# The memory turn of a recurrent attention kernel in two parts, with its sum copied on ScalarE, and another choice of streamed weight blocks

## The chip, the cores and the metric

The kernel runs on one core of a Trainium2 chip. The metric is the device time of one execution in microseconds (us), the median of several runs. The engines are TensorE (PE; its weight loads are PEld), VectorE (DVE), ScalarE (ACT), GpSimd (POOL) and SyncE (SP), which here only issues transfers. Tensors in HBM reach the on-chip memory SBUF by DMA; matmul results lie in PSUM until ACT or DVE copies them out.

## The reference

Two attention branches read the same `x` (2048 tokens, 640 wide) and a gate mixes them. Branch A is causal attention with 32 heads of 20 over a window of 256. Branch B is what the change touches: 64 segments of 32 tokens, one after the other, each with 8 memory tokens that the segment before has left.

```python
for s in range(n_seg):                       # 64, seg_len 32
    xs = x[:, s*seg_len:(s+1)*seg_len, :]
    h = concatenate([mem, xs], axis=1)       # 8 + 32 tokens
    q, k, v = h @ Wq, h @ Wk, h @ Wv         # 640 -> 32 heads x 192
    p = softmax(where(mask, q k^T * scale, -1e9))
    o = einsum('bhte,hed->btd', p v, Wo)     # back to 640
    mem = o[:, :M, :]                        # M = 8
    outs.append(o[:, M:, :])
return g * a + (1 - g) * concatenate(outs)   # g = sigmoid(sum(x * gate_w))
```

Only the memory ties a segment to the next, so branch B is a chain of 64 steps.

## The kernel before

Branch A runs first. In the same stretch and just after it the kernel projects the last eight tokens of each segment for q, k and v (class `Tail`), and loads weights. Then `branch_B` runs the 64 segments.

The four weights of branch B hold 84 blocks: for q, k and v four head groups of five blocks (one per slice `kt` of the 640 inputs, 128 x 1536 bf16, 384 KB), for the output projection o four groups of six (128 x 1280, 320 KB). [...] The table `STREAMED` names 21 blocks that are read from HBM again in every segment; the other 63 stay resident. A streamed block lands in a slot of the ring `b_w`, which has `RING = 5` slots. The load of a block is issued by SP once the last matmul on the block five places earlier has ended. SP issues the loads in the order of their use (`Weights.load`, L517 for blocks that are one transfer, L521 for o blocks 0, 2, 3 and 5; blocks 1 and 4 of o would be two).

Each segment follows the list `STEP` on PE, which is written out by hand: `k0 q0 k1 tk0 tq0 q1 s0 ... v3 p3 oa2 pv3 ob2 oa3 ob3 m`. `k0`, `q0`, `v0` are projections of a head group (`chunk`, L773; five slices `kt` of four matmuls that run side by side), `tk`/`tq` turns of the tokens, `s` scores, `p` the turn of the probabilities, `pv` the values (L935, L942), `oa`/`ob` two halves of an output group (L968), and `m` the memory turn. `Sched.run` plans the other engines from durations and dependences; SP and PE keep the given order.

At a segment's end stands this chain. The output sum of the segment lies in PSUM (`o_b`). DVE copies it to SBUF (`osum`, a buffer of the tag `OT`, L977). In `finish`, ten small matmuls turn the memory tokens (L989, `mem_ps`). DVE copies the result into the eight memory columns of the next segment's input `hT` (L994). Then `k0` of the next segment starts (L773). POOL stores the rest of `osum`, loads the branch A share and writes the output; `mix` runs on DVE in the next segment.

Of the kernel before, what the change touches and what calls it, by code (L numbers as in the profile page):

```python
# [8 lines left out]
FP32 = mybir.dt.float32  # L9
BF = mybir.dt.bfloat16  # L10
ALU = mybir.AluOpType
ACT = mybir.ActivationFunctionType
# [3 lines left out]
MEM = 8  # L16
# [377 lines left out]
P = 128  # L394
KT = 5
D = 640
# [273 lines left out]
def branch_B(ctx, tc, xin, mem0, weights, ring, c, omg_sb, ga_dram, b_dram, outf, hold, held, rest):  # L670
    nc = tc.nc
    nseg = xin.shape[0]
    scale = float(192) ** -0.5
    still, ident, mask, mk_m, mk_x, mk_z = c.still, c.ident, c.mask, c.mk_m, c.mk_x, c.mk_z
    kept = KEPT

    sb = {
        "w": (RING, [P, PIECE]), "tok": (3, [P, 384]), "vtok": (1, [P, 384]), "K02": (1, [P, 4, 2, L]),
        "PTm": (1, [P, 2, 4, L]), "Pm": (1, [P, 4, SEG]), "xg": (2, [P, 2, 12, MEM]), "xv": (1, [P, 384]), "hT": (2, [P, KT, SEG]),
# [6 lines left out]
    sc = Sched({"rest": len(held)} | {t: n for t, (n, _) in sb.items()} | {t: n for t, (n, _) in kept.items()} | ps)  # L686

    def tile_of(b, shape=None, dtype=BF, name=None):
        t = b["tag"]
        if b["tile"] is None:  # L690
            if t in kept:
                b["tile"] = still[t][b["n"] % kept[t][0]]
            elif t in sb:
                b["tile"] = pools[t].tile(sb[t][1], BF, name=f"b_{t}", tag=t)
            else:
                b["tile"] = pools[t].tile(shape, dtype, name=name or f"p_{t}", tag=t)
        return b["tile"]

    def load_x(s):
        hb = sc.buf("hT")  # L700

        def f():
            nc.gpsimd.dma_start(tile_of(hb)[:].rearrange("p k t -> p (k t)"), xin[s, :, 0:KT * SEG])
        return hb, sc.op("POOL", 540, 5000, f, writes=[hb])
# [16 lines left out]
    def pieces(kind, g, ms=range(5)):  # L721

        out = {}
        for m in ms:
            u = (kind, g, m)
            if u in weights.streamed:
                b = out[m] = sc.buf("w")
                sc.op("SP", 0.753 * weights.width(kind), 3000, lambda b=b, u=u: weights.load(u, tile_of(b)[:, 0:weights.width(u[0])], nc.sync), writes=[b])
        return out

    def w_of(kind, g, m, bufs):
        return bufs[m]["tile"] if m in bufs else weights.tiles[kind, g, m]
# [15 lines left out]
    hts = {0: load_x(0)}  # L748
# [3 lines left out]
    def f_m0():  # L752
        t = tile_of(tp, [P, KT, MEM], BF, "tp0")
        for kt in range(KT):
# [4 lines left out]
          writes=[hts[0][0]], after=[hts[0][1]])  # L759
# [192 lines left out]
    def oproj(kind, s, g):  # L952

        ms = PARTS[kind]
        OT = made["O", s, g]
        if g == 0 and kind == "oa":
            obufs[s] = sc.buf("o")
        o_b = obufs[s]
        wb = pieces("o", g, ms)

        def f(m):
            t = tile_of(o_b, [P, 512], FP32, "ps_o")
            for n in range(2):
                i, b = divmod(2 * m + n, 3)
                c = (4 * b + i) * L
                for h in range(2):
                    w = w_of("o", g, m, wb)[:, n * D + h * (D // 2):n * D + (h + 1) * (D // 2)]
                    nc.tensor.matmul(t[64 * h:64 * h + 64, 0:D // 2], lhsT=OT["tile"][:, c:c + 64], rhs=w,  # L968
                                     start=(g == 0 and m == 0 and n == 0), stop=(g == 3 and m == 5 and n == 1),
                                     tile_position=(0, 64 * h), skip_group_check=True)  # L970
        for m in ms:
            sc.op("PE", 273, 200, lambda m=m: f(m), reads=[OT] + [wb[n] for n in wb if n == m] + [slow[u] for u in slow if s == 0 and u == ("o", g, m)],
                  writes=[o_b], name=("o", s, g, m), mode=64)
        if g < 3 or kind == "oa":
            return
        osum = sc.buf("OT")
        sc.op("DVE", 492, 55, lambda: nc.vector.tensor_copy(tile_of(osum)[:, 0:D // 2], o_b["tile"][:, 0:D // 2]), reads=[o_b], writes=[osum])  # L977
        made["osum", s] = osum

    def finish(s):  # L980

        osum = made.pop(("osum", s))
        b = sc.buf("tr")

        def f():
            t = tile_of(b, [P, KT, MEM], FP32, "mem_ps")
            for kt in range(KT):
                for h in range(2):
                    nc.tensor.matmul(t[64 * h:64 * h + 64, kt, :], lhsT=osum["tile"][:, kt:D // 2:KT], rhs=ident[:, 64 * h:64 * h + MEM],  # L989
                                     start=(kt == 0), stop=True, tile_position=(0, 64 * h), skip_group_check=True)  # L990
        sc.op("PE", 360, 222, f, reads=[osum], writes=[b], name=("m", s), mode=64)
        if s + 1 < nseg:
            hT, xl = hts[s + 1]
            sc.op("DVE", 200, 55, lambda: nc.vector.tensor_copy(tile_of(hT)[:, :, 0:MEM], b["tile"][:]), reads=[b], writes=[hT], after=[xl])  # L994
        ga, rows = sc.buf("ga"), slice(s * SEG, (s + 1) * SEG)
        half = lambda t, h: t[rows, h * (D // 2):(h + 1) * (D // 2)]
        mine = lambda t, h: t[64 * h + MEM:64 * h + L, 0:D // 2]
        for h in range(2):
            sc.op("POOL", 500, 3000, lambda h=h: nc.gpsimd.dma_start(half(b_dram, h), mine(osum["tile"], h)), reads=[osum])
            sc.op("POOL", 500, 5000, lambda h=h: nc.gpsimd.dma_start(mine(tile_of(ga), h), half(ga_dram, h)), writes=[ga])  # L1000

        def mix(after):
            def f_r():
                nc.vector.scalar_tensor_tensor(out=ga["tile"][:], in0=osum["tile"][:, 0:D // 2], scalar=omg_sb[:, s:s + 1], in1=ga["tile"][:],  # L1004
                                               op0=ALU.mult, op1=ALU.add)
            sc.op("DVE", 552, 60, f_r, reads=[osum], writes=[ga], after=[after])
            for h in range(2):
                sc.op("POOL", 500, 3000, lambda h=h: nc.gpsimd.dma_start(half(outf, h), mine(tile_of(ga), h)), reads=[ga])  # L1008
        made["mix"] = mix
        if s + 1 == nseg:  # L1010
            mix(None)
# [3 lines left out]
    for n in names:  # L1015
        kind, s = n[:2]
        if s not in tails:
            tails[s] = load_tail(s)
            if s + 1 < nseg:
                hts[s + 1] = load_x(s + 1)  # L1020
        if kind == "m":
            finish(s)
        elif kind in "qkv":
            chunk(kind, s, n[2])
        elif kind in PARTS:
            oproj(kind, s, n[2])
        else:
            make[kind](s, n[2])
    with tc.manual_schedule():
        parts = []  # L1030
        for n in names:
            if n[0] in PARTS:
                parts += [("o",) + n[1:] + (m,) for m in PARTS[n[0]]]
            elif n[0] in KINDS:
                parts += [n + (m,) for m in range(KT)]
            else:
                parts.append(n)
        return sc.run([("m0", 0)] + parts)


PARTS = {"oa": range(3), "ob": range(3, 6)}
RING = 5
EARLY = 24
LAST = 11
HOLD = 5
DENSE = 8
STREAMED = {"q": ((1,), (1,), (2,), (1,)),
            "k": ((0,), (3,), (3,), (3,)),
            "v": ((4,), (0, 4), (0, 3), (3,)),
            "o": ((2,), (2, 5), (0, 3), (2, 5))}  # L1050


@with_exitstack
def kernel(
# [31 lines left out]
    allp = [(k, g, m) for k in KINDS for g in range(4) for m in range(6 if k == "o" else 5)]  # L1086
    streamed = [(k, g, m) for k, g, m in allp if m in STREAMED[k][g]]
    weights = Weights(tc, B_Wq, B_Wk, B_Wv, B_Wo, streamed)
# [6 lines left out]
    units = [lambda u=u: weights.load_resident(pre, u, nc.sync) for u in early]  # L1095
    ring = wctx.enter_context(tc.tile_pool(name="b_w", bufs=RING))
    first = {}
# [78 lines left out]
    with ExitStack() as bctx:  # L1176
        rest = bctx.enter_context(tc.tile_pool(name="b_rest", bufs=1))
        branch_B(bctx, tc, xin, mem0, weights, ring, step_c, omg_sb, ga_dram, b_dram, outf, holds[0], last[HOLD:], rest)
# [41 lines left out]
```

## Time and profile before

| | |
|---|---|
| median of 5 runs | 2080.93 us (2071.89 to 2084.55) |
| the profiled execution | 2063.62 us, its span 2061.9 us |
| busy: PE, DVE, ACT, POOL | 1915.6, 1047.9, 920.5, 727.2 us |
| first and last start of the memory copy L994 | 466.8 and 2029.5 us, 63 copies |
| moved by DMA | 593.83 MB, mean 288 GB/s over the span |

The segments fill the span from about 440 us on. PE is busy for 93% of the span, but its matmuls are pipelined and their ends are modelled, so this is no statement that PE works at its peak. The waits that count are those of PE; DVE, ACT and POOL are idle for half the time. One loop of the chain from copy L994 to the next takes (2029.5 - 466.8) / 62 = 25.2 us.

### The profile page before, as it was taken

Reading aid. Unit: us, or ns where it says so; the run is one execution under the profiler, and the core shown is the slowest. Engines: PE = TensorE matmul, PEld = TensorE weight load, DVE = VectorE, ACT = ScalarE, POOL = GpSimd, SP = SyncE. Lnnn points to the kernel's source line nnn. Section 1 sums busy time; section 2 is a strip of 40 time slices with the busy share of each in tenths; the row PEclk is TensorE's granted clock in tenths of the full one; section 3 lists DMA queues with packets and bytes.
Section 4 is the critical chain, followed back from the end, with each engine's and each line's share of the span. In section 5 each row is a group of like instructions: output and inputs, shape, how many; then the busy total and the mean of one; then the engine's idle time right before and its main releaser. Section 6 shows DMA issues by size and latency. Waiting matters only on the chain.

```text
span 2061.9 us, 92142 instructions
## 1 busy us (share of the span) xinstructions
PE 1915.6 (93%) x39670; PEld 1409.8 (68%) x39670; DVE 1047.9 (51%) x3338; ACT 920.5 (45%) x1885; POOL 727.2 (35%) x2008
## 2 busy tenths in 40 slices
PE   7999999989999999999999999999999999999997
PEld 6878878756666666666666666666666666666665
DVE  4888853334444445444445544444444444444444
ACT  3888832234444444444444444444444443444443
POOL 4222121233333334333343333333333333333332
PEclk8999999999999999999999999999999999999999
DMA  4232139789999999999999999999999999999997
GB/s 138 78 88 72 45 96 351 203 274 317 328 335 329 332 336 337 331 324 326 334 335 336 337 339 332 330 332 333 330 327 333 330 332 306 332 323 332 335 330 261
DMA packets 251153, 593.83 MB, mean 288 GB/s; under 512 B 39528, under 2 KB 59120, under 8 KB 250736
## 3 DMA queue, kind: packets, MB, share of 16 engines
q1 hardware_dynamic: 219248, 540.07, 75.2%
q0 software_dynamic: 31488, 47.78, 8.7%
q8 instruction: 313, 5.13, 1.0%
q14 instruction: 104, 0.85, 0.1%
HBM read 558.33 MB, written 29.37 MB: 285 GB/s over the span
## 4 chain that ended last, share of the span: by engine, by line
PE 60%; DMA 24%; issue 7%; DVE 5%; ACT 3%; SPq 0%; POOL 0%; POOLq 0%; DVEq 0%; ACTq 0%
DMA b_w<-in_B_Wo_dram 11%; PE ps_q L773 10%; PE ps_k L773 10%; DMA b_w<-in_B_Wv_dram 9%; PE ps_o L968 8%; PE ps_v L773 6%; PE t_psum L584 4%; PE qk_ps L138 3%; PE t_psv L602 2%; DMA b_w<-in_B_Wk_dram 2%; PE tr_q L797 2%; PE S_ps L853 2%; PE tr_k L797 2%; PE s_ps L236 2%; PE ps_pv L935 2%
## 5 line engine op out<-in xcount | busy, mean ns | idle before, releaser
L773 PEld LDWEIGHTS <-b_hT 128*32 128x32 bf16 x15360 | 372.6, 96 | 263.6 <-issue 50.6
L968 PEld LDWEIGHTS <-b_OT 128*64 128x64 bf16 x6144 | 370.4, 110 | 57.2 <-issue 32.5
L784 ACT CAST b_tok<-ps_k 128x384 bf16<-128x384 f32 x256 | 122.6, 479 | 340.4 <-PE ps_k L773 331.8
L773 PE MATMUL ps_q<-w_q,b_hT 128*32 128x384 bf16 x4096 | 257.4, 329 | 0.8 <-issue 0.8
L773 PE MATMUL ps_k<-w_k,b_hT 128*32 128x384 bf16 x4096 | 245.5, 328 | 0.0
L968 PE MATMUL ps_o<-hold,b_OT 128*64 128x320 bf16 x2560 | 237.4, 301 | 0.0
L919 DVE TENSOR_TENSOR b_PTm<-PT_ps,marks 128x320 bf16<-128x320 f32 x256 | 125.9, 492 | 201.1 <-PE PT_ps L907 201.1
L968 PE MATMUL ps_o<-b_w,b_OT 128*64 128x320 bf16 x1792 | 206.5, 301 | 23.0 <-DMA b_w<-in_B_Wo_dram 21.3
L824 DVE TENSOR_TENSOR b_Kz<-tr_k,marks 128x256 bf16<-128x256 bf16 x256 | 108.1, 422 | 230.7 <-PE tr_k L797 223.2
L773 PE MATMUL ps_v<-w_v,b_hT 128*32 128x384 bf16 x3584 | 212.4, 327 | 0.0
L239 ACT ACTIVATE pt<-s_ps 128x1024 bf16<-128x1024 f32 x180 | 183.6, 1026 | 57.3 <-PE s_ps L236 54.1
L946 ACT CAST b_OT<-ps_pv 128x480 bf16<-128x480 f32 x256 | 143.2, 559 | 143.4 <-PE ps_pv L942 143.4
L784 ACT CAST b_vtok<-ps_v 128x384 bf16<-128x384 f32 x256 | 122.7, 479 | 153.4 <-PE ps_v L773 152.7
L718 POOL DMA_DIRECT2D b_xg<-xin x256 | 142.5, 557 | 83.8 <-POOL b_QT L810 51.7
L968 PE MATMUL ps_o<-w_o,b_OT 128*64 128x320 bf16 x1792 | 169.9, 300 | 0.0
L829 POOL COPY b_K<-b_xg 128x64 bf16<-128x64 bf16 x256 | 61.0, 238 | 298.6 <-PE S_ps L853 298.6
L806 ACT COPY b_QT<-tr_q 128x384 bf16<-128x384 bf16 x256 | 123.5, 483 | 86.5 <-PE tr_q L797 86.5
L784 ACT CAST b_tok<-ps_q 128x384 bf16<-128x384 f32 x256 | 123.1, 481 | 84.8 <-PE ps_q L773 84.7
L773 PE MATMUL ps_v<-b_w,b_hT 128*32 128x384 bf16 x1536 | 131.2, 331 | 25.7 <-DMA b_w<-in_B_Wv_dram 24.5
L1008 POOL DMA_DIRECT2D out_dram<-b_ga x128 | 63.7, 498 | 256.2 <-DVE b_ga L1004 246.4
L977 DVE CAST b_OT<-ps_o 128x320 bf16<-128x320 f32 x64 | 31.5, 492 | 210.2 <-issue 201.5
L797 PEld LDWEIGHTS <-b_tok 128*64 128x64 bf16 x3072 | 108.3, 110 | 41.1 <-issue 22.4
(141 smaller groups left out, 3715.8 us busy)
## 6 DMA issues: line engine op xcount, KB each, us to landing
b_w<-in_B_Wv_dram SPq DMA_DIRECT2D x384, 384.0 KB, 4.9
b_w<-in_B_Wo_dram SPq DMA_DIRECT2D x448, 320.0 KB, 4.7
b_w<-in_B_Wk_dram SPq DMA_DIRECT2D x256, 384.0 KB, 4.9
b_w<-in_B_Wq_dram SPq DMA_DIRECT2D x256, 384.0 KB, 5.0
xin<-hold POOLq DMA_DIRECT2D x8, 1536.0 KB, 12.3
b_xg<-xin POOLq DMA_DIRECT2D x256, 48.0 KB, 4.4
w_q<-in_B_Wq_dram SPq DMA_DIRECT2D x16, 384.0 KB, 3.9
w_k<-in_B_Wk_dram SPq DMA_DIRECT2D x16, 384.0 KB, 3.9
```

The source lines that it names most:

```text
L239: nc.scalar.activation(out=pt, in_=sp[:], func=ACT.Exp, scale=scale)
L584: self.nc.tensor.matmul(pt[:, bb, :], lhsT=w[kt][:, c:c + P], rhs=self.xTb[:, kt, t0:t0 + hs * MEM], start=(kt == 0), stop=(kt == KT - 1))
L718: sc.op("POOL", 540, 5000, lambda: nc.gpsimd.dma_start(tile_of(b)[:].rearrange("p i b t -> p (i b t)"), xin[s, :, c:c + 192]), writes=[b])
L773: nc.tensor.matmul(t[32 * j:32 * j + 32, 0:384], lhsT=tile_of(hT)[:, kt, :], rhs=w[:, j * 384:(j + 1) * 384], start=(kt == 0), stop=(kt == ...
L784: nc.scalar.copy(dst, src)
L797: nc.tensor.transpose(t[64 * a:64 * a + 64, k, :], tok["tile"][:, c:c + 64], ident[:], tile_position=(0, 64 * a))
L806: nc.scalar.copy(dst, tq["tile"][:].rearrange("p b (j t) -> p b j t", t=SEG))
L824: nc.vector.tensor_tensor(out=tile_of(Kz)[:, :, :, 0:SEG], in0=src, in1=mk_z.unsqueeze(1).unsqueeze(3).to_broadcast([P, 4, 2, SEG]), op=AL ...
L919: nc.vector.tensor_tensor(out=tile_of(PTm)[:], in0=src.to_broadcast([P, 2, 4, L]), in1=mk_m.unsqueeze(1).unsqueeze(3).to_broadcast([P, 2, ...
L946: sc.op("ACT", 560, 50, lambda: nc.scalar.copy(tile_of(OT)[:, 0:12 * L], o["tile"][:, 0:12 * L]), reads=[o], writes=[OT])
L968: nc.tensor.matmul(t[64 * h:64 * h + 64, 0:D // 2], lhsT=OT["tile"][:, c:c + 64], rhs=w, start=(g == 0 and m == 0 and n == 0), stop=(g == ...
L1008: sc.op("POOL", 500, 3000, lambda h=h: nc.gpsimd.dma_start(half(outf, h), mine(tile_of(ga), h)), reads=[ga])
```

## The change

Three edits, all in branch B.

1. The copy of the output sum moves from DVE to ACT.
2. The memory turn becomes two PE steps, one for slices 0 and 1, one for slices 2 to 4, each with its own PSUM buffer of the tag `tr` and its own DVE copy into `hT`.
3. `STREAMED` names other blocks. There are 21 as before, with the same count for each of q (4), k (4), v (6) and o (7), and all are one transfer.

```diff
-        sc.op("DVE", 492, 55, lambda: nc.vector.tensor_copy(tile_of(osum)[:, 0:D // 2], o_b["tile"][:, 0:D // 2]), reads=[o_b], writes=[osum])
+        sc.op("ACT", 430, 50, lambda: nc.scalar.copy(tile_of(osum)[:, 0:D // 2], o_b["tile"][:, 0:D // 2]), reads=[o_b], writes=[osum])
...
-        b = sc.buf("tr")
-
-        def f():
-            t = tile_of(b, [P, KT, MEM], FP32, "mem_ps")
-            for kt in range(KT):
-                for h in range(2):
-                    nc.tensor.matmul(t[64 * h:64 * h + 64, kt, :], lhsT=osum["tile"][:, kt:D // 2:KT], rhs=ident[:, 64 * h:64 * h + MEM],
-                                     start=(kt == 0), stop=True, tile_position=(0, 64 * h), skip_group_check=True)
-        sc.op("PE", 360, 222, f, reads=[osum], writes=[b], name=("m", s), mode=64)
-        if s + 1 < nseg:
-            hT, xl = hts[s + 1]
-            sc.op("DVE", 200, 55, lambda: nc.vector.tensor_copy(tile_of(hT)[:, :, 0:MEM], b["tile"][:]), reads=[b], writes=[hT], after=[xl])
+
+        def turn(i, kts):
+            b = sc.buf("tr")
+
+            def f():
+                t = tile_of(b, [P, KT, MEM], FP32, "mem_ps")
+                for kt in kts:
+                    for h in range(2):
+                        nc.tensor.matmul(t[64 * h:64 * h + 64, kt, :], lhsT=osum["tile"][:, kt:D // 2:KT], rhs=ident[:, 64 * h:64 * h + MEM],
+                                         start=(kt == kts[0]), stop=True, tile_position=(0, 64 * h), skip_group_check=True)
+            sc.op("PE", 72 * len(kts), 222, f, reads=[osum], writes=[b], name=("m", s, i), mode=64)
+            if s + 1 < nseg:
+                hT, xl = hts[s + 1]
+                c = slice(kts[0], kts[-1] + 1)
+                sc.op("DVE", 150, 55, lambda: nc.vector.tensor_copy(tile_of(hT)[:, c, 0:MEM], b["tile"][:, c]), reads=[b], writes=[hT], after=[xl])
+        for i, kts in enumerate(TURNS):
+            turn(i, kts)
...
+TURNS = (range(2), range(2, KT))
...
-STREAMED = {"q": ((1,), (1,), (2,), (1,)),
-            "k": ((0,), (3,), (3,), (3,)),
-            "v": ((4,), (0, 4), (0, 3), (3,)),
-            "o": ((2,), (2, 5), (0, 3), (2, 5))}
+STREAMED = {"q": ((0,), (0, 3), (), (4,)),
+            "k": ((0,), (0,), (0,), (2,)),
+            "v": ((1, 4), (4,), (1, 4), (4,)),
+            "o": ((2, 3), (3,), (0, 3), (0, 3))}
```

In `STREAMED` each of the four tuples is a head group, and the numbers are the slices that are streamed.

More of the change, by code (lines that the diff above doesn't have):

```diff
@@ L1035, in branch_B @@
                 parts += [n + (m,) for m in range(KT)]
+            elif n[0] == "m":
+                parts += [n + (i,) for i in range(len(TURNS))]
             else:
```

## The prediction, made before the changed kernel ran

> **What bounds the kernel now.** I read the page first, for who waits for whom, then the busy time by stages, then the transfers, then two places on the time line. From the page's groups (busy us and mean ns, then idle time before the group and what ended it):
>
> ```profile
> L946 ACT CAST b_OT<-ps_pv 128x480 bf16<-128x480 f32 x256 | 143.2, 559 | 143.4 <-PE ps_pv L942 143.4
> L784 ACT CAST b_vtok<-ps_v 128x384 bf16<-128x384 f32 x256 | 122.7, 479 | 153.4 <-PE ps_v L773 152.7
> ...
> L977 DVE CAST b_OT<-ps_o 128x320 bf16<-128x320 f32 x64 | 31.5, 492 | 210.2 <-issue 201.5
> ```
>
> Two ACT copies out of PSUM give ACT's slope, and the DVE copy that moves has its duration. The stages, one row each with busy time of PE, PEld, DVE, ACT, POOL, then clock, DMA share, GB/s:
>
> ```profile
> 350.00:440.00 90.00, 88.94 (x737) 62.79 (x738) 31.22 (x70) 28.26 (x71) 25.88 (x46) 1.00 0.72 209
> 467.00:972.00 505.00, 468.82 (x10524) 336.31 (x10528) 243.48 (x861) 211.76 (x480) 193.78 (x562) 1.00 0.96 330
> ```
>
> In the segments two things are near their limit together: PE, idle for 36.2 us of 505 (1.8 us of a 25.2 us segment), and the DMA engines, busy for 96%. So a gap that PE loses can come back as a wait for weights. The tile `b_w`, engine waits and time to landing:
>
> ```profile
>   PE ps_v L773: 24.5, 45
>   PE ps_o L968: 21.3, 41
>   PE ps_k L773: 5.6, 9
> ...
>   PE ps_q L773: 0.5, 3
> ...
> DMA to landing us min/median/max: 3.3/4.9/7.4
> ```
>
> Weights are late for v and o, hardly for k and q. Last, the time line at a segment's end and at a late weight (start, duration, what ended the idle time):
>
> ```profile
> 1417.99 0.44 PE L968 MATMUL ps_o<-b_w,b_OT 128*64 128x320 bf16 x4
> 1418.52 0.49 DVE L977 CAST b_OT<-ps_o 128x320 bf16<-128x320 f32 x1 [2.90 <-issue]
> ...
> 1419.07 0.54 PE L989 MATMUL mem_ps<-ident,b_OT 128*64 128x8 bf16 x10 [0.65 <-DVE b_OT L977]
> ...
> 1419.65 0.20 DVE L994 CAST b_hT<-mem_ps 128x40 bf16<-128x40 f32 x1 [0.64 <-PE mem_ps L989]
> ...
> 1420.00 0.35 PE L773 MATMUL ps_k<-b_w,b_hT 128*32 128x384 bf16 x4 [0.39 <-DVE b_hT L994]
> ```
>
> ```profile
> 1409.53 0.35 PE L773 MATMUL ps_v<-b_w,b_hT 128*32 128x384 bf16 x4
> 1409.70 0.50 PE L773 MATMUL ps_v<-w_v,b_hT 128*32 128x384 bf16 x8
> 1410.72 0.35 PE L773 MATMUL ps_v<-b_w,b_hT 128*32 128x384 bf16 x4 [0.52 <-DMA b_w<-in_B_Wv_dram]
> ```
>
> The turn costs 1420.00 - 1418.43 = 1.57 us from the last output matmul's end to `k0`. In the second, group v2 uses two streamed blocks that are 0.49 us of PE work apart, and the second is late.
>
> **Waits for weights, place by place.** A pause of under 0.35 us hides beneath the pipelined matmul before it, so I took from the matmul records, over 61 segments, the mean start-to-start time ahead of each of the 21 places beyond its 8th percentile. The sum is 1.26 us a segment. Three places hold 0.716 of it: v1 block 4 (0.207), v2 block 3 (0.242), oa2 block 0 (0.267); the other 18 share 0.543, 0.030 each. PE work from one streamed block to the next: a q, k or v block takes 0.163 us, an o block 0.27 (both from time line steps), plus what stands between. The three places are just those that follow their predecessor by under 0.7 us (0.65, 0.49, 0.61). The landings say why: a 384 KB block lands a median 0.96 us after its predecessor where the two were issued 0.8 to 1.0 us apart, and 1.06 where they were issued over 1.8 us apart. Blocks land one after the other, at least 0.93 us apart (10th percentile; 0.79 for o), whatever SP does. The 4.9 us to landing is mostly a queue.
>
> [...]
>
> **The change part by part.**
> *Sum on ACT.* ACT's slope is (559 - 479) / (480 - 384) = 0.83 ns, so 128x320 takes 479 - 64 x 0.83 = 426 ns, 66 less than 492. ACT to weight load took 51 ns at L968, DVE to weight load 53 at L989: no difference. ACT's next work is `k0`'s copy, 0.8 us after `k0` starts, so it is hidden; were it not, it would delay `tk0`. POOL's store of `osum` waits for ACT now; that is 66 ns earlier. `mix` reads it over 2 us later.
> *Turn in two.* Ten matmuls take 0.54 us, the last 0.217, so they start 36 ns apart; the first four end after 3 x 36 + 217 = 325 ns, 215 earlier. The first copy has 16 elements per partition instead of 40; with DVE's slope (492 - 200) / 280 = 1.04 ns it takes 175, 25 less. The second copy (24 elements, 183 ns) starts 1.15 us after the last output matmul and ends at 1.33; `k0`'s third slice is due at 1.26 + 2 x 0.163 = 1.59 and, by L994 to matmul 0.15, can start at 1.48. Hidden, with 0.11 us to spare. The built program has the two waits apart, ahead of slice 0 and of slice 2. DVE's extra copy meets no other work for 2 us. The second `tr` buffer's last reader ended long before. PE does the same ten matmuls.
> Together 66 + 215 + 25 = 306 ns of 1.57 us; x 63 = 19.3 us if nothing gives it back.
> *Other blocks.* Bytes and transfers stay: 21 per segment, 14 x 384 + 7 x 320 KB. SP still issues 21; in its order a v and an o load change places, POOL's queue is unchanged. What changes is when a block is wanted. By the same count, pairs under 0.7 us apart become six: q1 0-3, v0 1-4, v2 1-4 and q3 4 to k3 2 (0.49 each), oa0 2 to ob0 3 (0.61), v3 4 to oa2 0 (0.45). In time the blocks are bunched more than before. In the change's favour speaks the round of five slots: from a block to the one five later it is at least 5.1 us (before 4.5), and ahead of the six second blocks 5.5 to 5.9 us, where the three late ones had 4.5 to 5.2. After the turn, five blocks are wanted within 3.5 us (before 4.9), while five landings take about 5.
> Bounds: as costly as before, 6 x 0.24 + 15 x 0.03 = 1.89, +0.63 us a segment. If the rounds alone decided, nearly all places fall to 0.03 and two (rounds of 5.1 and 5.2) keep 0.1: 0.77, -0.49. I take 0.20 for a close pair, since landings in a row decide more than rounds, but rounds are longer: 6 x 0.20 + 15 x 0.03 = 1.65, +0.39.
> *Given back.* A shorter turn makes all 21 blocks due sooner, DMA being busy for 96%. Bounds: none, or all 0.31. I take 0.17, a little over half: the turn is where the ring refills, and blocks one to five after it come closest now.
> *Outside the segments.* From 350 to 440 us PE is busy for 88.9 of 90 us and DMA for 72%; q and k of group 1 need three streamed blocks there, of group 2 one, where both had two. Nothing, at most 2 us either way.
>
> Sum: +0.39 - 0.306 + 0.17 = +0.25 us a segment, x 63 = +16 us. On the profiled execution's own time 2063.6 + 16 = 2079.6; it lies 17 us under the median of the runs shown, and the same 16 on the median gives 2080.9 + 16 = 2097 us.
>
> **Rivals.**
> *A, faster: the rounds decide.* If time from issue to landing stays near 4.9 us whatever the order, waits fall by 0.49 and the turn keeps its 0.31: -0.80 x 63 = -50 us, 2031. Half of it, or the turn's gain alone with the waits unchanged (-19), gives about 2055 to 2062. For it: each of the three late places has a short round. Against: three other rounds of 5.1 us (ahead of blocks in oa2 to ob3) show under 0.04 us of wait, and landing gaps that ignore issue gaps.
> *B, no change.* Close pairs cost 0.16 and the turn gives half back: 6 x 0.16 + 0.45 - 1.26 = +0.15, -0.15: 2081.
> *C, slower still.* Close pairs cost 0.24 and DMA takes the whole turn: +0.63 x 63 = +40, 2121. The point from which it decides is DMA's 4% of idle time running out.
> *D, the change doesn't do what it says:* if slice 0 waited for both copies, 1.57 us would lose only 66 ns less the second copy's start. The built program's separate waits speak against it; under 0.05.
>
> **How the numbers follow.** A measurement tells about 0.5% (10 us) from no change. Forecast (+10 to +28 us) 0.42, C and between 0.16, B with D 0.22, A 0.20. Slower 0.58, same 0.22, faster 0.20. The likeliest case has 2091 to 2109; for 8 in 10 the range goes to C's end and into A's weaker half, 2060 to 2122.
>
> **What would show it.** Sum copy on ACT near 426 ns; start of `k0` 1.26 us after the last output matmul. Waits for `b_w` move to q and k (q from 0.5 us to over 10), those of o fall, all together rise by a quarter or more; v2's wait stays. DMA share up, segment 25.45 us. Wrong if the waits for weights fall (A), or if the median time to landing doesn't move while close pairs aren't late.

## The result, and the profile after

The changed kernel takes 2094.94 us (median of 24 runs), the kernel before on the same chips 2074.75 (45 runs). The ratio is 1.0093, with a 95% interval of 1.0076 to 1.0109: 0.9% slower, about 19 us. The profiled execution took 2081.45 us against 2063.62, +17.8; the forecast was +16. Executions of one kernel scatter (2059 to 2093 us before), and these two lie 11 and 13 us under their medians, so what is read below from single profiled executions is good to some 0.2 us a segment.

From the groups of instructions of the changed kernel, the sum's copy and the memory copies (busy us and mean ns, then idle time before and what ended it):

```profile
L977 ACT CAST b_OT<-ps_o 128x320 bf16<-128x320 f32 x64 | 27.3, 426 | 135.8 <-PE ps_o L968 135.8
...
L997 DVE CAST b_hT<-mem_ps 128x16 bf16<-128x16 f32 x126 | 22.5, 179 | 251.2 <-PE mem_ps L991 247.9
```

The sum's copy takes 426 ns, as forecast from ACT's slope. The two memory copies mix to 179; apart they take 175 and 183.

The busy time by stages of the changed kernel, in the segments (PE, PEld, DVE, ACT, POOL, clock, DMA share, GB/s):

```profile
467.00:972.00 505.00, 471.64 (x10484) 333.64 (x10480) 236.56 (x859) 219.76 (x499) 192.72 (x559) 1.00 0.96 329
972.00:1476.00 504.00, 469.45 (x10412) 330.82 (x10412) 234.79 (x854) 217.89 (x495) 191.64 (x557) 1.00 0.95 327
```

DMA moves slightly less in the same time (before 330 and 335 GB/s). PE's busy time over the two stages hardly changes (941.1 us, before 941.8): the turn's idle time falls, that for weights rises, and a wait that hides beneath the matmul before it (a record of L773 lasts 0.33 us in the mean, while on the time line below the matmuls after `k0`'s first four start 0.18 us after those) doesn't count as idle there (waits of 1.26 us a segment before show as 51.9 / 63 = 0.82 us of idle time).

The tile `b_w` of the changed kernel, who waited for it and its time to landing:

```profile
  PE ps_k L773: 30.1, 62
  PE ps_v L773: 18.0, 41
  PE ps_o L968: 11.2, 19
  PE ps_q L773: 9.2, 24
...
DMA to landing us min/median/max: 3.4/5.0/7.5
```

The waits have moved from v and o to k and q, and grown in sum from 51.9 to 68.5 us. k waits 62 times, where it waited 9 times. The turn and what follows it, one segment on the time line of the changed kernel:

```profile
1455.66 0.47 PE L968 MATMUL ps_o<-w_o,b_OT 128*64 128x320 bf16 x4
...
1456.21 0.43 ACT L977 CAST b_OT<-ps_o 128x320 bf16<-128x320 f32 x1 [2.10 <-PE ps_o L968]
...
1456.69 0.54 PE L991 MATMUL mem_ps<-ident,b_OT 128*64 128x8 bf16 x10 [0.57 <-ACT b_OT L977]
...
1457.05 0.41 DVE L997 CAST b_hT<-mem_ps 128x16 bf16<-128x16 f32 x2 [3.87 <-PE mem_ps L991]
...
1457.28 0.35 PE L773 MATMUL ps_k<-b_w,b_hT 128*32 128x384 bf16 x4
1457.46 0.82 PE L773 MATMUL ps_k<-w_k,b_hT 128*32 128x384 bf16 x16
...
1458.11 0.34 PE L773 MATMUL ps_q<-b_w,b_hT 128*32 128x384 bf16 x4
...
1459.61 0.35 PE L773 MATMUL ps_k<-b_w,b_hT 128*32 128x384 bf16 x4 [0.52 <-DMA b_w<-in_B_Wk_dram]
```

`k0` starts at 1457.28, while the second memory copy still runs (1457.05 + 0.41 = 1457.46): the turn in two does what it says. From the last output matmul's end to `k0` the median over all segments is 1.16 us, before 1.48. Then `k0`, `q0` and `k1` each begin with a streamed block, 0.82 us of PE work apart, and the third isn't there. So 0.32 us is won at the turn, and more is lost just after it and at v2. By start-to-start times, as in the forecast, the waits for weights went from 1.26 to 1.71 us a segment (at `k1` the 8th percentile is itself a wait: it is 0.26 us there and 0.15 with the old turn, so that 1.71 is some 0.1 low), and the segment from 25.20 to 25.53. The segment grew by 0.32 while the turn gave 0.32, so 0.64 us were lost elsewhere; the waits by place account for 0.45, or 0.56 with that correction.

### The profile page after: what moved, and what is told of

Its sections match the earlier page's. It is cut to its first block, busy times and chain, and to the rows that moved or that the text cites. A ratio compares the mean times of both kernels' runs of the same rounds, so it can differ in the third digit from the quotient of the medians.

```text
span 2079.7 us, 92207 instructions
## 1 busy us (share of the span) xinstructions
PE 1931.6 (93%) x39670; PEld 1404.1 (68%) x39670; DVE 1026.7 (49%) x3337; ACT 947.9 (46%) x1949; POOL 726.2 (35%) x2008
## 4 chain that ended last, share of the span: by engine, by line
PE 56%; DMA 36%; DVE 4%; ACT 2%; issue 1%; SPq 0%; POOL 0%; POOLq 0%; ACTq 0%
DMA b_w<-in_B_Wv_dram 13%; PE ps_o L968 12%; DMA b_w<-in_B_Wk_dram 10%; DMA b_w<-in_B_Wq_dram 8%; PE ps_v L773 7%; PE ps_q L773 7%; PE ps_k L773 6%; DMA b_w<-in_B_Wo_dram 5%; PE t_psum L584 5%; PE qk_ps L138 3%; PE t_psv L602 2%; PE S_ps L853 2%; PE ps_pv L935 2%; PE s_ps L236 2%; PE tr_q L797 1%
## 5 line engine op out<-in xcount | busy, mean ns | idle before, releaser
L773 PEld LDWEIGHTS <-b_hT 128*32 128x32 bf16 x15360 | 371.0, 96 | 309.8 <-issue 75.2
L968 PE MATMUL ps_o<-hold,b_OT 128*64 128x320 bf16 x2560 | 245.9, 299 | 0.0
L773 PE MATMUL ps_q<-w_q,b_hT 128*32 128x384 bf16 x4096 | 225.7, 329 | 0.0
L773 PE MATMUL ps_k<-w_k,b_hT 128*32 128x384 bf16 x4096 | 223.5, 328 | 0.0
L968 PE MATMUL ps_o<-b_w,b_OT 128*64 128x320 bf16 x1792 | 206.8, 302 | 11.6 <-DMA b_w<-in_B_Wo_dram 11.2
L773 PE MATMUL ps_v<-w_v,b_hT 128*32 128x384 bf16 x3584 | 213.1, 328 | 0.0
L773 PE MATMUL ps_v<-b_w,b_hT 128*32 128x384 bf16 x1536 | 130.0, 328 | 19.8 <-DMA b_w<-in_B_Wv_dram 18.0
L997 DVE CAST b_hT<-mem_ps 128x16 bf16<-128x16 f32 x126 | 22.5, 179 | 251.2 <-PE mem_ps L991 247.9
## 6 DMA issues: line engine op xcount, KB each, us to landing
xin<-hold POOLq DMA_DIRECT2D x8, 1536.0 KB, 11.2
```

Of the source, the lines that this page charges most:

```text
L773: nc.tensor.matmul(t[32 * j:32 * j + 32, 0:384], lhsT=tile_of(hT)[:, kt, :], rhs=w[:, j * 384:(j + 1) * 384], start=(kt == 0), stop=(kt == ...
```

## The experiments

All ratios are to the kernel before on the same chip, with 95% intervals. "Waits" are the start-to-start waits ahead of streamed blocks, a segment's mean over 61 segments of the profiled execution: at each place, what it takes beyond its quickest cases.

**The turn alone.** The changed kernel with the old table.

```diff
-STREAMED = {"q": ((0,), (0, 3), (), (4,)),
-            "k": ((0,), (0,), (0,), (2,)),
...
+STREAMED = {"q": ((1,), (1,), (2,), (1,)),
+            "k": ((0,), (3,), (3,), (3,)),
...
```

> The turn in two and the sum on ACT, with the old table of streamed blocks. Theory (blocks land one after the other, so part of a shorter turn comes back as waits for weights): the turn is 0.31 us shorter, the waits grow by 0.1 to 0.17 us a segment, net -0.14 to -0.21 us x 63 = 9 to 13 us faster than before (0.5%). Rival, nothing comes back: 19 us faster (0.9%). Rival, all comes back: no change.

Measured 2060.26 us, ratio 0.9950 (0.9929 to 0.9971): 10 us faster. The turn is short (median 1.16 us), and the waits rise to 1.55 us. Where before `b_w` was late for k 9 times and for q 3 times, it is 14 and 6 times:

```profile
  PE ps_k L773: 10.9, 14
...
  PE ps_q L773: 4.1, 6
```

By the medians about half of the 19 us comes back as waits for weights. The profiled executions alone would say nearly all (waits +0.29 us, segment 25.20 to 25.18), but that of the kernel before lies 11 us under its median and this one 1.5; the medians decide.

**The table alone.** The kernel before with the new table.

> The new table alone, with the old turn on DVE. Theory: the waits for weights rise from 1.26 to about 1.65 us a segment, +0.39 x 63 = 25 us slower than before (1.2%), with the waits at v2 and in the run k0, q0, k1, q1 after the turn. Rival, the rounds of five slots decide: waits fall by up to 0.49 us, up to 31 us faster. Rival, the table is neutral and the changed turn is what costs: no change.

Measured 2100.45 us, ratio 1.0131 (1.0094 to 1.0168): 27 us slower. Waits 1.76 us, the largest at v2's second block (0.44) and at `k1` (0.41). Who waited for `b_w`:

```profile
  PE ps_v L773: 27.6, 53
  PE ps_k L773: 22.7, 43
```

The rounds of five slots, which the new table makes longer ahead of its close pairs, don't decide.

**One block moved inside the run after the turn.**

```diff
-            "k": ((0,), (0,), (0,), (2,)),
+            "k": ((0,), (3,), (0,), (2,)),
```

> The changed kernel with one block of its table exchanged: k1 streams slice 3 in place of slice 0, 0.49 us of PE work later, so that after the turn the blocks are wanted 0.82, 1.30 and 0.88 us apart in place of 0.82, 0.81 and 1.37. Theory (a run of blocks wanted faster than they land is what makes k1 late): the wait at k1, about 0.5 us a segment in the changed kernel, falls by 0.3 or more, some of it comes back at q1 (second block 0.49 after the first), net -0.1 to -0.25 us, 6 to 16 us faster than the changed kernel. Rival (only pairs under 0.7 us apart wait): the same time as the changed kernel.

Measured 2097.94 us, ratio 1.0110 (1.0074 to 1.0147), no faster than the changed kernel. The expected gain isn't there, as the rival said; but the rival's reason isn't right either, since `k1` waits though it follows its predecessor by 0.81 us. Who waited for `b_w` in this kernel:

```profile
  PE ps_q L773: 29.2, 60
...
  PE ps_k L773: 15.3, 33
```

Against the changed kernel k's wait halved and q's tripled. By place, `k1` fell from 0.44 to 0.20 us, and the two blocks of `q1` rose from 0.04 and 0.21 to 0.13 and 0.48. In both kernels five blocks, from `k0` to the second of `q1`, are wanted within 3.49 us of PE work. Moving one inside that stretch moved the wait to the next, and all waits together rose to 2.08 us.

**A table spread in time, with the new turn.**

```diff
+STREAMED = {"q": ((3,), (2,), (0,), (0,)),
+            "k": ((0,), (4,), (0,), (1,)),
+            "v": ((2,), (0, 4), (0, 4), (2,)),
+            "o": ((2,), (2, 5), (2, 5), (2, 5))}
```

> The new turn with another table: q slices 3, 2, 0, 0; k 0, 4, 0, 1; v 2, (0,4), (0,4), 2; o 2, (2,5), (2,5), (2,5). From k0 to v1 the blocks are wanted 0.9 to 1.3 us apart, close pairs are two in v1 and v2 (0.65) and one in oa2. Theory: waits for weights about as in the kernel before with the new turn, 1.2 to 1.4 us a segment; 9 to 16 us faster than before, within 6 us of the old table with the new turn. If evenness in the first half of the segment were all that counts: 20 us faster or more.

Measured 2046.49 us, ratio 0.9889 (0.9845 to 0.9933): 23 us faster than before (14 to 32 by the interval), where 9 to 16 were expected. The middle value is in the range of the expectation's other case (20 us or more, evenness alone); the interval reaches into both. It is the fastest version with whole blocks, and beats both kernels. The wanted times are 0.98 to 1.34 us apart from `k0` to `v1`; the first five blocks span 4.54 us. The busy time by stages of this kernel:

```profile
467.00:972.00 505.00, 475.25 (x10673) 341.31 (x10669) 240.20 (x872) 224.40 (x508) 195.82 (x567) 1.00 0.97 334
972.00:1476.00 504.00, 476.87 (x10726) 343.46 (x10723) 242.61 (x883) 225.38 (x511) 197.78 (x575) 1.00 0.97 337
```

Who waited for `b_w`:

```profile
  PE ps_v L773: 17.3, 25
  PE ps_o L968: 14.7, 30
  PE ps_k L773: 10.0, 17
...
  PE ps_q L773: 4.6, 10
```

The DMA engines move more in the same time than in either kernel (337 against 335 and 327 GB/s in the second stage): it is the same 8.3 MB a segment, in segments of 24.85 us against 25.20 and 25.53. The waits are 1.23 us with the short turn. (The sentence of the expectation on a close pair in oa2 miscounts: there are only the two in v1 and v2.)

**The same table with the old turn.**

> The spread table (q slices 3, 2, 0, 0; k 0, 4, 0, 1; v 2, (0,4), (0,4), 2; o 2, (2,5), (2,5), (2,5)) with the old turn on DVE. With the new turn it ran 1.1% faster than before, the old table with the new turn 0.5%. Theory (the table and the turn each act, the turn's gain is kept in part): 0.5 to 0.7% faster than before. Rival (the table only lets the turn's gain through whole): within 0.3% of before.

Measured 2059.89 us, ratio 0.9915 (0.9885 to 0.9946). That is 18 us faster (11 to 24), outside the rival's 0.3%, so by the middle values most of the 23 us is the table's. The interval overlaps that of the version with the new turn, so what the turn adds on top of this table (5 us by the middle values) isn't settled.

**Half the new table, twice.** The changed kernel with the old rows for q and k, and its mirror with the old rows for v and o.

> The changed kernel with the old rows for q and k and the new rows for v and o. Summing the waits place by place: the q and k places waited 1.07 us a segment in the changed kernel and 0.33 with the new turn and the old table, the v and o places 0.75 and 1.22. If places only add up, this mixture waits 0.33 + 0.75 = 1.08 us, 0.47 less than the old table with the new turn: about 2030 us, 2.0% faster than before. Rival, the queue of landings carries over from one half of the segment to the next, so that neither half's waits stay what they were: a time between the old table with the new turn and the changed kernel, -0.5% to +0.9%.

> The mirror: the changed kernel with the old rows for v and o and the new rows for q and k. If places add up: 1.07 + 1.22 = 2.29 us of waits a segment, 0.47 more than the changed kernel, about 2.4% slower than before. Rival, carried over: between -0.5% and +0.9%.

Measured 2088.84 us, ratio 1.0078 (1.0056 to 1.0100), and 2096.46 us, ratio 1.0082 (1.0055 to 1.0110). Adding up places fails both times. With the old q and k rows the v and o places should have kept 0.75 us; they have 1.33, and all waits 1.95 us (1.08 expected). In the mirror all waits are 2.06 (2.29 expected), and the time is far from 2.4% slower. Both times lie in the rival's range. That fits a queue that goes from one half of the segment into the other, which no run here isolates; shown is that this table can't be judged row by row.

**Half the bytes.** Every streamed block is loaded by half, and the matmuls read the loaded half twice, in the kernel before and in the changed one. The result leaves out the other half of each streamed block, while PE's work stays.

```diff
-                sc.op("SP", 0.753 * weights.width(kind), 3000, lambda b=b, u=u: weights.load(u, tile_of(b)[:, 0:weights.width(u[0])], nc.sync), writes=[b])
+                sc.op("SP", 0.753 * weights.width(kind), 3000, lambda b=b, u=u: weights.load(u, tile_of(b)[:, 0:weights.width(u[0]) // 2], nc.sync, 2), writes=[b])
...
-                nc.tensor.matmul(t[32 * j:32 * j + 32, 0:384], lhsT=tile_of(hT)[:, kt, :], rhs=w[:, j * 384:(j + 1) * 384],
+                i = j % 2 if kt in wb else j
+                nc.tensor.matmul(t[32 * j:32 * j + 32, 0:384], lhsT=tile_of(hT)[:, kt, :], rhs=w[:, i * 384:(i + 1) * 384],
...
```

> The kernel before with every streamed block loaded by half (the first half of its columns; the matmuls on the other half read the first again, so PE's work stays, and the values of the streamed blocks' second halves are left out). DMA moves about 240 MB less. Theory: the waits for weights, 1.26 us a segment, all but vanish: 64 x 1.2 = 77 us less, about 1995 us. Rival, the pauses at those places are not waits for weights: unchanged within 10 us.

> The changed kernel with the same halved loads (values left out in the same way). Theory (the table costs only through the queue of landings): the table's cost is gone and the turn's 0.31 us is kept whole, so 0.31 x 63 = 19 us faster than the halved kernel before. Rival (the table or the turn costs something else on PE): as slow as the halved kernel before or up to 20 us slower.

Measured 1977.02 us and 1956.62 us, ratios 0.9514 (0.9480 to 0.9548) and 0.9419 (0.9385 to 0.9452): the changed kernel is now 20.4 us faster, all that the turn was to bring. The tile `b_w` of the halved kernel before:

```profile
DMA to landing us min/median/max: 2.1/2.7/4.6
```

Its first stage in the segments, in the columns used before:

```profile
467.00:972.00 505.00, 484.88 (x11122) 349.74 (x11120) 257.46 (x911) 223.80 (x508) 205.15 (x595) 1.00 0.65 185
```

And all that TensorE still waits for `b_w` in the halved changed kernel:

```profile
  DMA b_w<-in_B_Wv_dram: 1.8, 1
```

With the DMA share at 0.65 (0.63 in the halved changed kernel) a halved block lands after 2.7 us (2.8), where a whole one took 4.9 at 0.96, the waits are under 0.02 us a segment in both, and the segments take 23.93 and 23.61 us: 0.32 apart, just what the turn is shorter by. From the kernel before to its halved form the segment loses 25.20 - 23.93 = 1.27 us, its 1.26 us of waits; the medians differ by 96 us, the profiled executions by 84.5, where 77 was expected. With the loads out of the way the two kernels differ by just the turn, so the table costs nothing but waits for weights.

## Why the prediction was right

*Direction and size.* Forecast +16 us, 2097; measured +0.93%, +19 us, 2095, and +17.8 between the profiled executions. The likeliest case held. That 2097 comes within 2 us of 2095 is in part luck: it was built on the first five runs, whose median (2080.9) lies 6 us over that of all 45.

*The turn.* 66 + 215 + 25 = 306 ns; measured by the medians of 63 segments 66 + 227 + 25 ns, 0.32 us in all, every copy as worked out (426, 175, 183 ns). The segment that the forecast took as its sample was not the usual one: there `k0` began 0.15 us after the copy's end and the turn took 1.57 us, where the medians are 0.055 and 1.48, so `k0` began at 1.16 us and not at 1.26. What the turn is shorter by is untouched by that. The weight load waited 51 ns on ACT's copy, as forecast. The second copy stayed hidden: in the median it ends 0.18 us after `k0` has begun.

*The table.* Forecast +0.39 us, 25 us; the table alone measured 27 us (20 to 35 by the interval). The sum was right, but the rule under it was not, so this part is luck: one error of 0.40 us and one of 0.46 cancelled. "Close pairs wait 0.20 each, other places 0.03" gave 1.20 + 0.45; in the changed kernel the six close pairs waited 0.80 us together (0.13 each: v2 0.31 and q1 0.21, the rest 0.04 to 0.10), and the other fifteen places 0.91. The largest wait of all, 0.44 us at `k1`, is at a place 0.81 us after its predecessor, which the rule put at 0.03. The forecast had named the cause beside the rule (five blocks wanted within 3.5 us, while five landings take about 5), but counted it only under what the turn gives back. The moved block showed that right after the turn the stretch counts, and not the pair. (By start times v3's block and that of oa2 are 0.5 us apart before and 0.33 after, where the forecast counted 0.61 and 0.45; its list of close pairs stays the same.) Set side by side:

| kernel | turn | first five blocks wanted within | their waits |
|---|---|---|---|
| before | old | 4.87 us | 0.16 us |
| old table | new | 4.87 us | 0.33 us |
| spread table | new | 4.54 us | 0.28 us |
| new table | old | 3.49 us | 0.63 us |
| changed | new | 3.49 us | 0.86 us |
| changed, `k1` moved | new | 3.49 us | 0.97 us |
| new q and k rows, old v and o rows | new | 3.49 us | 0.67 us |
| old q and k rows, new v and o rows | new | 4.87 us | 0.44 us |

(PE work without waits; the waits are the sum over these five places, a segment's mean.)

The stretch alone doesn't set the wait. In the changed kernel the five blocks from `k2` to k3 are wanted within 3.57 us too, and wait 0.20 us together. Two things differ there: no block is wanted in the 2.3 us before `k2`, and the blocks land 0.96 to 1.05 us apart, where `k0` and `k1` land 1.9 and 1.5 us after the block before them (medians). What holds those two up, slots that come free late or POOL's own transfers, which take 17% of the DMA engines' time in the first microsecond after the memory copy, no run here tells apart.

*Given back.* Forecast 0.17 of 0.31 us. With the old table the turn brought 10 us of 19 (6 to 15), so about half came back; with the new table it brought 8 us by the middle values (1.0131 to 1.0093), and with half the bytes, at a DMA share of 0.65 and 0.63, nothing came back (20.4 us were won). Here, then, the gain was eaten by the load on DMA: with the load taken away it came through whole. An estimate from the traces suggests why: by the times of their packets, summed and shared out over 16, the DMA engines are busy for 24.3 us a segment before, 24.4 in the changed kernel and 24.0 with the spread table, while PE, when no weight is late, needs 23.93 us with the old turn and 23.61 with the new (the halved kernels). By this estimate the transfers were already the longer of the two, and a shorter turn could only use what slack the table leaves. No run here tests that bound.

*DMA share: wrong.* The forecast had it rise. It fell from 0.96 and 0.97 to 0.96 and 0.95. Five slots are all that can be loaded ahead. Folding the DMA packets' times over the segments of the changed kernel, in half-microsecond slices from the start of the first memory copy, the share is 1.01 to 1.02 from 1 to 5 us, down to 0.82 to 0.89 between 21 and 22.5 us, and 0.82 and 0.87 in the last two slices before the next copy. In the kernel before it is 0.83 in one slice (from 8.5 us), and 0.88 to 1.02 in all others. The bunched blocks were late in one stretch and left the engines less to do in another.

*Time to landing: wrong.* The forecast took the 4.9 us for mostly a queue. In the kernel before, the fifteen 384 KB blocks of q and k that are loaded between 60 and 230 us, where the DMA share is 0.26, land after a median 3.3 us. By this comparison about 1.6 us of the 4.9 come with the load on DMA, not most of it.

*What would show it.* o's waits fell (21.3 to 11.2 us), and the sum rose by a third; q's rose to 9.2 us, short of the 10 named, and k's more than any. v2's wait, which was to stay, rose (second block 0.24 to 0.31 us). The segment is 25.53 us, forecast 25.45. One sign of being wrong came close: the median time to landing hardly moved (4.9 to 5.0 us), and four of the six close pairs waited 0.10 us or less. It points where the rule on close pairs failed.

*The rivals.* A (rounds decide) falls with the table alone. B (no change) and C (2121 us) lie outside the interval. D falls with the time line, where `k0` starts before the second copy ends.

## What to carry to other kernels

When weights stream through a few buffers and DMA is near its limit (a share of 0.96 here), write down when PE wants each block, and compare every stretch of as many blocks as there are buffers with the time in which that many land (here five, about 5 us by landing gaps of 0.96 to 1.06 us). A stretch that is clearly shorter is where to look: here the one after the turn (3.49 us) made PE wait 0.86 us a segment, and moving one block inside it moved the wait. It doesn't say how long the wait is; a stretch as short later in the segment (3.57 us) cost a quarter as much (0.20 us). Evenness in a list of blocks is not evenness in time. A ring with more slots was not tried. Before a pause on PE is shortened, ask what it was hiding, and compare the DMA engines' time with PE's own: here about half of a clean 0.3 us went back to DMA, and the whole of it came through only with half the bytes, at a DMA share of 0.63 to 0.65 instead of 0.95 to 0.97.

## What the runs showed of the hardware that was not expected

- Time to landing was not one figure: in the kernel before, a 384 KB block landed after a median 3.3 us at a DMA share of 0.26 and 4.9 at 0.96, a 320 KB block after 4.7 there. With every streamed block half as large, at a share of 0.65, it was 2.7 us, and the minimum fell from 3.3 to 2.1; load and size changed together in that run.
- At a DMA share of 0.95 to 0.96 landings didn't follow the issues: in the changed kernel, 384 KB blocks issued about 0.5 us apart (0.4 to 0.6) landed a median 1.1 us apart, and so did those issued over 1.8 us apart.
